# Query features made transposed and spread over the partitions by DMA, in place of transposes on TensorE

## The chip, the core and the metric

The kernel runs on one core of one Trainium2 chip. The metric is the device time of one execution in microseconds (us). Engines are named as the profile names them: PE is TensorE (PEld its weight loads), DVE is VectorE, ACT is ScalarE, POOL is GpSimd, and SP issues the DMAs (SPq is its queue).

## The reference

Three layers follow each other on 4 batches of 1088 rows: linear attention with 4 heads of 32, then two feed-forward blocks. The change touches the attention only:

```python
def phi(x):
    a = np.einsum('rd,bhsd->bhsr', S1, x)          # r = 8
    b = np.einsum('rd,bhsd->bhsr', S2, x)
    return np.einsum('bhsi,bhsj->bhsij', a, b).reshape(*x.shape[:-1], 64)
q_p, k_p = (phi(q), phi(k))
kv = np.einsum('bhsf,bhsd->bhfd', k_p, v);  z = np.sum(k_p, axis=2)
num = np.einsum('bhsf,bhfd->bhsd', q_p, kv)
den = np.einsum('bhsf,bhf->bhs', q_p, z)[..., None] + 1e-06
return num / den
```

Then `x` goes through `relu(xk @ w_k)**2 @ w_v`, gated by a sigmoid, and through a block with a 1088 x 1088 spatial product. All data are float32.

## The kernel before

**Chunks.** Each batch is cut into three chunks of 384, 384 and 320 rows, so there are 12 chunks, i = 0 to 11; batch b has the chunks 3b to 3b + 2. Work on a chunk's queries has four parts. `q_feat` (L229) makes the features: three matmuls (L188) with 128 rows of q each as the stationary operand give the 64 numbers a and b per row, ACT copies them out of PSUM (L191 or L196, shown by the profile as L114, the line of the helper), and DVE or POOL forms the 256 products a_i b_j (L199); the list `QP` gives chunks 3, 4, 6, 9 and 10 to POOL, the others to DVE. There a row of q lies on a partition and the features along it. `q_turn` (L233) turns that round: six transposes on PE against a unit matrix (L240) and two copies by ACT (L242) put features on partitions. `q_num` (L249) multiplies with the masked k-v sums (L257, six matmuls), divides (L261 to L263), and `q_out` (L266) transposes the result (L275) into the layout of the next layer.

**The loop.** The first feed-forward block runs in 96 steps g, eight for each chunk. Step g does `up(g)` (three matmuls, L336 by the helper at L111; Relu on ACT, L339; for even g the square on POOL, L342), `down(g - 4)` (L385 or L111) and `sqsplit(g - 1)` (ACT L371 or L359, DVE L117). A product in "three matmuls" splits both operands into a high and a low part; a plain float32 matmul (L385, L188, L257) shows as two records in the profile. All other work is hung on steps by `plan(g, fn)`: the four query parts of chunk j at `QS[j]` and after it, two steps apart, the key features and sums of a batch, `load_q`, `load_k`, and the loads and splits of the spatial weights wT (`wstep`: SP loads a 128 x 384 piece into one of two buffers `st0`, `st1`, ACT copies it and DVE or POOL subtracts, L117).

**Order.** The program is built with a scheduler that simulates a timeline and then writes each engine's queue in its own order. Each engine runs its queue strictly in that order and waits where an operand or a buffer isn't ready. So `plan` gives priorities, and the engine's row order is what counts. All DMAs go out from SP, so a transfer that waits for a buffer holds back each later one. PE has eight PSUM banks; the query parts use banks 4 to 7.

**Memory.** `VR` is one tile of nine pieces of 128 x 512. The query parts use pieces 0 to 5 of it (transposed features in 0 to 3, quotients in 4 and 5) until step 72, from which on the second block uses all of them. `n1L` holds the product of `q_feat`.

Of the kernel before, what the change touches and what calls it, by code (L numbers as in the profile page):

```python
# [8 lines left out]
F32 = mybir.dt.float32  # L9
# [3 lines left out]
ALU = mybir.AluOpType  # L13
# [29 lines left out]
KP = (6, 10)  # L43
QJ = (0, 0, 4, 1, 0, -4, -1, 0, 2, 2, 0, -8)
PG = 1
ES = 93
EP = 2
G2 = 96
# [18 lines left out]
def attn_moe_gmlp(ctx: ExitStack, tc: tile.TileContext, qT, kT, va, st, wk, wv, wr, win, wout,  # L67
                  wT, wtail, btail, mu, ident, msk, out):
    nc = tc.nc
    TE, VE, SE, GE = nc.tensor, nc.vector, nc.scalar, nc.gpsimd  # L70

    pool = ctx.enter_context(tc.tile_pool(name="sb", bufs=1))
    pp = ctx.enter_context(tc.tile_pool(name="ps", bufs=1, space=PSUM))

    uid = [0]

    def sb(tag, shape, dt=F32):
        uid[0] += 1
        return pool.tile(shape, dt, tag=tag, bufs=1, name=f"{tag}_{uid[0]}")
# [7 lines left out]
    def rot(*tags):  # L87
        i = count.get(tags, 0)
        count[tags] = i + 1
        return tags[i % len(tags)]  # L90
# [117 lines left out]
    def k_sum(b, g, ts=range(NT)):  # L208
# [12 lines left out]
        if g == 1:  # L221
# [4 lines left out]
                                         .to_broadcast([128, 2 * nh, HD + 1]), op=ALU.mult)  # L226
            kbd[b] = kb.rearrange("p (g h) c -> p g (h c)", g=2)

    def q_feat(i):  # L229
        qp = qst[i] = sb("n1L", [128, 3, 256])  # L230
        features(q_s[i // 3], i % 3, qp, 4, GE if i in QP else None)

    def q_turn(i):  # L233
        c = i % 3
        n = CH[c][1]
        qp, qt = qst[i], []
        for g in range(2):
            pt = bank(6 + g)
            for t in order3(c):
                TE.transpose(pt[:, cut(c, t)], qp[:, t, 128 * g:128 * g + 128], idn)  # L240
            q2 = vr(rot(0, 1, 2, 3), CMAX)
            copy(q2[:, :n], pt[:, :n])  # L242
            qt.append(q2)
        qst[i] = qt
# [396 lines left out]
    def plan(g, fn, *a):  # L641
        todo.setdefault(g, []).append(lambda: fn(*a))

    def gated(fn):
        return wraps(fn)(lambda *a: behind(prep_0, fn, *a))
# [4 lines left out]
    for j in range(1, NI):  # L650
        sp = 1 if j < 3 else 2
        for n, fn in enumerate((q_feat, q_turn, q_num, q_out)):
            plan(QS[j] + sp * n, gated(fn) if j < 3 and n == 0 else fn, j)
        e = QS[j] + 3 * sp
        plan(max(8 * j - 6, e + 1), prep, j)
        plan(max(8 * j - 4, e + 2), prep_r, j)
        plan(8 * j - 2, receive, j)
        plan(8 * j - 1, gate, j)
# [23 lines left out]
    def conv_late():  # L682
        behind(anchor[:1], conv64)

    for n in range(3):
        plan(R0[n], conv_first)
        if n < 2:
            plan(R0[n], total_wv, n)
# [122 lines left out]
```

## Time and profile before

| | |
|---|---|
| three runs | 474.23, 474.27 and 476.06 us, median 474.27 |
| profiled execution, whole | 475.52 us |
| its span, first to last instruction | 473.7 us |
| granted clock of TensorE, mean | 0.995 of full speed |
| PE busy over the span | 456.4 us (96%) |
| DVE, ACT, POOL busy | 235.6, 236.3, 189.9 us |
| hardware DMA queue | 12192 packets, 18.31 MB |

The span is shown by the profile in 40 slices and can be asked for stretch by stretch. It has three stages: the start with the first key features (0 to 40 us), the loop of 96 steps beside the remaining attention (40 to about 215 us), and the spatial products (215 us to the end). A group's row names a line, an engine and an operation, then output and input tiles. Matmuls overlap in the records, so PE's busy time is no sum of durations: the pace of PE is read from the starts of neighbouring rows, or from the chain that ended last, which counts each piece once.

### The profile page before, as it was taken

Reading aid. Unit: us, or ns where it says so; the run is one execution under the profiler, and the core shown is the slowest. Engines: PE = TensorE matmul, PEld = TensorE weight load, DVE = VectorE, ACT = ScalarE, POOL = GpSimd, SP = SyncE. Lnnn points to the kernel's source line nnn. Section 1 sums busy time; section 2 is a strip of 40 time slices with the busy share of each in tenths; the row PEclk is TensorE's granted clock in tenths of the full one; section 3 lists DMA queues with packets and bytes.
Section 4 is the critical chain, followed back from the end, with each engine's and each line's share of the span. In section 5 each row is a group of like instructions: output and inputs, shape, how many; then the busy total and the mean of one; then the engine's idle time right before and its main releaser. Section 6 shows DMA issues by size and latency. Waiting matters only on the chain.

```text
span 473.7 us, 7304 instructions
## 1 busy us (share of the span) xinstructions
PE 456.4 (96%) x2754; PEld 433.4 (91%) x2754; DVE 235.6 (50%) x433; ACT 236.3 (50%) x569; POOL 189.9 (40%) x247
## 2 busy tenths in 40 slices
PE   6987999989999999999999999999999999999997
PEld 5976899788998898899999999999999999999996
DVE  3778748788477774437552335621335521212121
ACT  2464687886786866876435423432523442311111
POOL 2447545576475785456325503341213440200000
PEclk9899999999999999999999999999999999999999
DMA  7952200112200000022000000000100000100001
GB/s 239 335 192 91 92 1 19 33 35 77 66 19 0 2 0 1 0 72 80 26 17 18 0 15 0 1 2 0 48 1 1 1 1 0 48 1 0 1 1 47
DMA packets 12228, 18.77 MB, mean 40 GB/s; under 512 B 1761, under 2 KB 10785, under 8 KB 12193
## 3 DMA queue, kind: packets, MB, share of 16 engines
q1 hardware_dynamic: 12192, 18.31, 12.3%
q8 instruction: 21, 0.34, 0.3%
q14 instruction: 15, 0.11, 0.1%
HBM read 16.08 MB, written 2.23 MB: 39 GB/s over the span
## 4 chain that ended last, share of the span: by engine, by line
PE 71%; DVE 9%; ACT 6%; DMA 5%; POOL 4%; issue 3%; SPq 1%; POOLq 0%; DVEq 0%; ACTq 0%
PE p L111 59%; DMA st<-in_wT_dram 3%; PE p L385 3%; DVE w L117 3%; PE p L219 2%; PE p L257 2%; PE p L507 2%; PE p L508 2%; ACT m L339 2%; DMA xs0H<-in_va_dram 2%; PE p L188 1%; DVE w L127 1%; ACT w L114 1%; DVE m L117 1%; ACT w L371 1%
## 5 line engine op out<-in xcount | busy, mean ns | idle before, releaser
L512 DVE TENSOR_TENSOR m<-p,m 128x384 f32<-128x384 f32 (+1 forms) x43 | 22.9, 532 | 96.9 <-PE p L508 92.7
L111 PE MATMUL p<-m,k 128*128 128x384 f32 (+1 forms) x288 | 65.4, 347 | 2.7 <-ACT m L339 2.7
L342 POOL TENSOR_TENSOR m<-m 128x384 f32<-128x384 f32 (+1 forms) x48 | 41.3, 863 | 46.9 <-ACT m L339 43.2
L499 ACT ACTIVATE m<-p 128x384 f32<-128x384 f32 (+1 forms) x44 | 20.6, 469 | 77.2 <-PE p L111 73.4
L111 PEld LDWEIGHTS p<-m,k 128*128 128x128 f32 x288 | 47.8, 189 | 6.9 <-ACT m L339 3.7
L111 PE MATMUL p<-w,m 128*128 128x384 f32 (+1 forms) x288 | 52.3, 327 | 0.0
L111 PE MATMUL p<-w,k 128*128 128x384 f32 (+1 forms) x288 | 51.6, 327 | 0.0
L111 PE MATMUL p<-w,n1H 128*128 128x384 f32 (+1 forms) x192 | 48.7, 330 | 1.0 <-DVE x L512 1.0
L111 PEld LDWEIGHTS p<-w,m 128*128 128x128 f32 x288 | 48.1, 188 | 0.5
L111 PE MATMUL p<-w,n0H 128*128 128x384 f32 (+1 forms) x192 | 48.2, 329 | 0.0
L111 PEld LDWEIGHTS p<-w,k 128*128 128x128 f32 x288 | 47.9, 188 | 0.3
L339 ACT ACTIVATE m<-p 128x384 f32<-128x384 f32 (+1 forms) x96 | 42.9, 473 | 9.5 <-PE p L111 8.9
L117 DVE TENSOR_TENSOR w<-m,w 128x384 fp32r<-128x384 f32 (+1 forms) x44 | 33.4, 771 | 26.5 <-ACT w L371 21.7
L117 DVE TENSOR_TENSOR m<-m,m 128x384 fp32r<-128x384 f32 (+1 forms) x47 | 27.2, 578 | 28.8 <-ACT m L114 27.6
L111 PEld LDWEIGHTS p<-w,n1H 128*128 128x128 f32 x192 | 34.2, 188 | 2.4 <-DVE x L512 1.3
L453 POOL TENSOR_SCALAR rs<-mv 128x1 f32<-128x1 f32 x34 | 8.4, 246 | 66.0 <-DVE mv L452 65.1
L111 PEld LDWEIGHTS p<-w,n0H 128*128 128x128 f32 x192 | 34.2, 188 | 0.5
L385 PE MATMUL p<-w,wvT 128*128 128x384 f32 (+1 forms) x88 | 34.5, 474 | 0.1
L447 ACT ACTIVATE VR<-p 128x512 f32<-128x512 f32 x34 | 20.2, 597 | 27.7 <-PE p L111 27.6
L111 PE MATMUL p<-w,n0L 128*128 128x384 f32 (+1 forms) x96 | 31.5, 328 | 0.0
L111 PE MATMUL p<-w,n1L 128*128 128x384 f32 (+1 forms) x96 | 31.5, 328 | 0.0
L455 DVE TENSOR_SCALAR VR<-VR,mv,rs 128x512 f32<-128x512 f32 x34 | 21.1, 621 | 20.4 <-POOL rs L454 20.4
(193 smaller groups left out, 1042.9 us busy)
## 6 DMA issues: line engine op xcount, KB each, us to landing
st<-in_wT_dram SPq DMA_DIRECT2D x16, 192.0 KB, 2.4
w<-in_kT_dram SPq DMA_DIRECT2D x8, 192.0 KB, 4.5
w<-in_qT_dram SPq DMA_DIRECT2D x8, 192.0 KB, 3.9
out_dram<-m SPq DMA_DIRECT2D x8, 192.0 KB, 1.9
st<-in_wT_dram SPq DMA_DIRECT2D x8, 160.0 KB, 2.3
xs0H<-in_va_dram SPq DMA_DIRECT2D x2, 528.0 KB, 7.0
xs0L<-in_va_dram SPq DMA_DIRECT2D x2, 528.0 KB, 4.4
w<-in_wk_dram SPq DMA_DIRECT2D x2, 512.0 KB, 6.2
```

Of the source, the lines that this page charges most:

```text
L111: TE.matmul(out_ap, lhsT=l, rhs=r, start=first and n == 0, stop=last and n == 2)
L117: return eng.tensor_tensor(out=L, in0=src, in1=H.bitcast(F32), op=ALU.subtract)
L219: TE.matmul(kv[:, w * g:w * g + w], lhsT=kp, rhs=vt if wide else vt[:, VP * g:VP * g + VP], start=(t == 0), stop=(t == NT - 1))
L257: nd_pe[0] = TE.matmul(o.rearrange("p h c -> p (h c)"), lhsT=qt[g][:, cut(c, t)], rhs=kb[:, g], start=not wide or g == 0, stop=not wide or ...
L339: SE.activation(out=r, in_=hk, func=AF.Relu)
L342: anchor[2] = GE.tensor_tensor(out=sq, in0=r, in1=r, op=ALU.mult)
L385: TE.matmul(vvs[i], lhsT=wvT[:, f // 2], rhs=hls.pop(g), start=f == 0, stop=f == NF - 1)
L447: SE.activation(out=v, in_=pv, func=AF.Relu)
L455: VE.tensor_scalar(out=v, in0=v, scalar1=mv[:, 0:1], scalar2=rs, op0=ALU.subtract, op1=ALU.mult)
L499: SE.activation(out=u, in_=pu, func=AF.Relu)
L507: TE.matmul(acc, lhsT=T2, rhs=wtile(NK, c)[1], start=False, stop=False)
L512: VE.tensor_tensor(out=u, in0=acc, in1=u, op=ALU.mult)
```

## The change

For chunks 3 to 11 (`SPREAD = 3`; batches 1 to 3) `q_feat` becomes `q_spread` and `q_turn` becomes `q_prod`; chunks 0 to 2 stay as they were. `q_order` copies the feature matrix once on POOL into an order by factor and head, so that one matmul with it as the stationary operand and the chunk's q as the moving one gives all a and b with their index on the partitions. ACT copies 96 of these rows into piece 8 of `VR`. SP writes them to DRAM (`far0` or `far1`), then reads them back six times with repeated rows: two transfers fill `fa` (each row of a eight times), four fill `fb` (the eight rows of b eight times). `q_prod` multiplies the two tiles in one instruction on POOL or DVE, by the same list `QP`. `fa` lies in pieces 0 and 1 or 2 and 3 of `VR`, `fb` in pieces 6 and 7 or in `n1L`, by turns. Chunks 3 to 9 have `q_spread` two steps earlier than `q_feat` was (`QE_ = 2`).

```diff
--- before.py
+++ after.py
@@ -43,6 +43,8 @@
 KP = (6, 10)
 QJ = (0, 0, 4, 1, 0, -4, -1, 0, 2, 2, 0, -8)
 PG = 1
+SPREAD = 3
+QE_ = 2
 ES = 93
 EP = 2
 G2 = 96
@@ -71,6 +73,8 @@
 
     pool = ctx.enter_context(tc.tile_pool(name="sb", bufs=1))
     pp = ctx.enter_context(tc.tile_pool(name="ps", bufs=1, space=PSUM))
+
+    dp = ctx.enter_context(tc.tile_pool(name="dr", bufs=1, space=bass.MemoryType.DRAM))
 
     uid = [0]
 
@@ -226,11 +230,48 @@
                                          .to_broadcast([128, 2 * nh, HD + 1]), op=ALU.mult)
             kbd[b] = kb.rearrange("p (g h) c -> p g (h c)", g=2)
 
+    Sq = [None]
+
+    def q_order():
+        t = sb("T12", [128, 2, 2 * NH, 8])
+        for x in range(2):
+            GE.tensor_copy(t[:, x], Sb[:, :, 8 * x:8 * x + 8])
+        Sq[0] = t.rearrange("p s h i -> p (s h i)")
+
+    def q_spread(i):
+        b, c = divmod(i, 3)
+        o, n = CH[c]
+        e = rot(1, 0)
+        pq = bank(6 + e)[:, :n]
+        TE.matmul(pq, lhsT=Sq[0], rhs=q_s[b][:, o:o + n], start=True, stop=True)
+        y = vr(8, n)[:96]
+        copy(y, pq[:96])
+        fa = VR[:, 2 * e:2 * e + 2, :n]
+        fb = VR[:, 6:8, :n] if e else sb("n1L", [128, 2, n])
+        far = dp.tile([96, n], F32, tag=f"far{e}", bufs=1, name=f"far_{i}")
+        nc.sync.dma_start(out=far, in_=y)
+        for h in range(NH):
+            r, g = 8 * h, h // 2
+            if h % 2 == 0:
+                nc.sync.dma_start(out=fa[:, g], in_=far[r:r + 16].unsqueeze(1).to_broadcast([16, 8, n]))
+            nc.sync.dma_start(out=fb[64 * (h % 2):64 * (h % 2) + 64, g],
+                              in_=far[64 + r:72 + r].unsqueeze(0).to_broadcast([8, 8, n]))
+        qst[i] = (fa, fb)
+
+    def q_prod(i):
+        fa, fb = qst[i]
+        (GE if i in QP else VE).tensor_tensor(out=fa, in0=fa, in1=fb, op=ALU.mult)
+        qst[i] = [fa[:, 0], fa[:, 1]]
+
     def q_feat(i):
+        if i >= SPREAD:
+            return q_spread(i)
         qp = qst[i] = sb("n1L", [128, 3, 256])
         features(q_s[i // 3], i % 3, qp, 4, GE if i in QP else None)
 
     def q_turn(i):
+        if i >= SPREAD:
+            return q_prod(i)
         c = i % 3
         n = CH[c][1]
         qp, qt = qst[i], []
@@ -650,7 +691,8 @@
     for j in range(1, NI):
         sp = 1 if j < 3 else 2
         for n, fn in enumerate((q_feat, q_turn, q_num, q_out)):
-            plan(QS[j] + sp * n, gated(fn) if j < 3 and n == 0 else fn, j)
+            early = QE_ if SPREAD <= j < 10 and n == 0 else 0
+            plan(QS[j] + sp * n - early, gated(fn) if j < 3 and n == 0 else fn, j)
         e = QS[j] + 3 * sp
         plan(max(8 * j - 6, e + 1), prep, j)
         plan(max(8 * j - 4, e + 2), prep_r, j)
@@ -682,6 +724,7 @@
     def conv_late():
         behind(anchor[:1], conv64)
 
+    plan(QS[SPREAD] - QE_ - 3, q_order)
     for n in range(3):
         plan(R0[n], conv_first)
         if n < 2:
```

In the built order the first place is PE behind the first Relu-square steps, about 40 to 47 us of the trace before. Before (`n1L_548` holds the product of chunk 3, `w_83` the q of batch 1, `kb` the k-v sums, `w_100` and so on the squares):

```order
L257 MATMUL p_164_585<-kb_54_209,VR_61 128x132 x6
L240 MATMUL p_170_612<-idn_62,n1L_548 128x128 x3
L240 MATMUL p_171_617<-idn_62,n1L_548 128x128 x3
L188 MATMUL p_203_712<-Sbd_119,w_83_320 128x128 x3
L385 MATMUL p_110_414<-w_100_379,wvT_79 128x384
L111 MATMUL p_110_414<-w_105_398,xs1L_78 128x384
L111 MATMUL p_110_414<-w_105_398,xs1H_77 128x384 x2
L385 MATMUL p_110_414<-w_111_418,wvT_79 128x384
L111 MATMUL p_110_414<-w_120_447,xs1L_78 128x384
L111 MATMUL p_110_414<-w_120_447,xs1H_77 128x384 x2
```
After (`T_116` is the ordered feature matrix, `w_83` and `w_155` the q of batches 1 and 2):

```order
L246 MATMUL p_188_674<-w_83_322,T_116_430 128x384
L192 MATMUL p_208_749<-Sbd_121,w_154_564 128x128 x3
L316 MATMUL p_106_403<-idn_64,VR_63 128x128 x3
L246 MATMUL p_206_737<-w_83_322,T_116_430 128x320
L115 MATMUL p_110_416<-w_92_348,xs1L_80 128x384
L115 MATMUL p_110_416<-w_92_348,xs1H_79 128x384 x2
L246 MATMUL p_275_975<-w_155_568,T_116_430 128x384
L298 MATMUL p_163_593<-kb_54_211,VR_63 128x132 x6
L192 MATMUL p_255_908<-Sbd_121,w_154_564 128x128 x3
L426 MATMUL p_110_416<-w_100_381,wvT_81 128x384
```
The six transposes and three feature matmuls of a chunk have gone, and the single matmuls of chunks 4, 5 and 6 (each on line 246) now stand close together, far ahead of the `kb` products that need them.

The second place is SP, from the second load of `win` on. Before (`wT` pieces go into `st`):

```order
L147 DMA w_205_719<-in_win_dram 128x1024
L147 DMA w_252_877<-in_win_dram 128x1024
L147 DMA w_288_998<-in_wout_dram 128x1024
L173 DMA w_237_828<-in_qT_dram 128x384 x2
L173 DMA w_237_828<-in_qT_dram 128x320
L412 DMA st_365_1247<-in_wT_dram 128x384
L412 DMA st_349_1204<-in_wT_dram 128x384
L412 DMA st_387_1323<-in_wT_dram 128x384
L412 DMA st_420_1418<-in_wT_dram 128x384
L412 DMA st_455_1530<-in_btail_dram 128x384
```
After (`far_513` belongs to chunk 3, `far_678` to chunk 4):

```order
L151 DMA w_201_722<-in_win_dram 128x1024
L252 DMA far_513<-VR_63 96x384
L151 DMA w_242_865<-in_win_dram 128x1024
L256 DMA VR_63<-far_513 128x1x384
L257 DMA VR_63<-far_513 64x1x384 x2
L256 DMA VR_63<-far_513 128x1x384
L257 DMA VR_63<-far_513 64x1x384 x2
L252 DMA far_678<-VR_63 96x384
L177 DMA w_229_825<-in_qT_dram 128x384 x2
L177 DMA w_229_825<-in_qT_dram 128x320
L256 DMA VR_63<-far_678 128x1x384
L257 DMA n1L_677<-far_678 64x1x384 x2
```
Between the two loads of `win` and behind them stand now the write and the six reads of each chunk in turn; the q of batch 3 (`w_229`) is loaded between chunk 4's write and its reads.

The third place is SP further on, among the `wT` loads. Before:

```order
L412 DMA st_401_1364<-in_wT_dram 128x384
L412 DMA st_576_1938<-in_wT_dram 128x384
L412 DMA st_436_1470<-in_wT_dram 128x384
L412 DMA st_589_1977<-in_wT_dram 128x384
L427 DMA st_575_1935<-in_wtail_dram 64x384
L412 DMA st_606_2033<-in_wT_dram 128x384
L412 DMA st_583_1960<-in_wT_dram 128x384
```
After (`far_1502` is chunk 9, `far_1640` chunk 11, `far_1661` chunk 10, `far_1358` chunk 8):

```order
L453 DMA st_350_1233<-in_wT_dram 128x384
L257 DMA VR_63<-far_1502 64x1x384
L252 DMA far_1640<-VR_63 96x320
L252 DMA far_1661<-VR_63 96x384
L256 DMA VR_63<-far_1358 128x1x320 x2
L453 DMA st_337_1198<-in_wT_dram 128x384
L257 DMA n1L_1639<-far_1640 64x1x320 x4
L453 DMA st_370_1300<-in_wT_dram 128x384
L256 DMA VR_63<-far_1502 128x1x384
L453 DMA st_402_1399<-in_wT_dram 128x384
L256 DMA VR_63<-far_1502 128x1x384
L453 DMA st_436_1513<-in_btail_dram 128x384
```
The `wT` loads that followed each other now stand between reads that fill `VR` or `n1L` and so wait for an earlier chunk to have left its buffer.

The fourth place is POOL, at the first products. Before:

```order
L199 TENSOR_TENSOR n1L_548<-sab_553 128x768
L680 TENSOR_TENSOR wvT_79<-xs1H_77,xs1L_78 128x256
L296 TENSOR_TENSOR m_112_420<-x_59_232 128x384
L680 TENSOR_TENSOR wvT_79<-xs1H_77,xs1L_78 128x256
L199 TENSOR_TENSOR n0H_564<-sab_569 128x768
L199 TENSOR_TENSOR n1L_711<-sab_716 128x768
L117 TENSOR_TENSOR xrL_453<-mx_450,xrH_452 128x384
L342 TENSOR_TENSOR m_162_578<-m_161_576 128x384
```
After:

```order
L337 TENSOR_TENSOR m_112_422<-x_59_234 128x384
L722 TENSOR_TENSOR wvT_81<-xs1H_79,xs1L_80 128x256
L263 TENSOR_TENSOR VR_63<-VR_63 128x2x384
L121 TENSOR_TENSOR xrL_458<-mx_455,xrH_457 128x384
L263 TENSOR_TENSOR VR_63<-VR_63,n1L_677 128x2x384
L383 TENSOR_TENSOR m_161_586<-m_160_584 128x384
L121 TENSOR_TENSOR xrL_474<-mx_471,xrH_473 128x384
L383 TENSOR_TENSOR m_144_529<-m_143_527 128x384
```
The products of chunks 3 and 4 (line 263) stand behind the sums `wvT` and ahead of the squares (lines 342 before, 383 after).

## Rows read from the trace of the kernel before

**Rows 1.** Stretches: length, then busy PE, PEld, DVE, ACT, POOL, clock, DMA share, GB/s
```profile
40.00:150.00 110.00, 105.27 (x678) 94.20 (x677) 78.65 (x130) 81.46 (x205) 65.80 (x64) 1.00 0.14 41
...
215.00:473.70 258.70, 255.44 (x1518) 251.48 (x1516) 91.95 (x184) 86.85 (x201) 66.58 (x97) 1.00 0.04 14
```

**Rows 2.** PE's waits from 36 to 160 us: total, times, longest
```profile
PE p L111 <- ACT m L339: 2.7, 4, 1.3
PE p L275 <- DVE VR L263: 1.6, 2, 1.4
PE p L188 <- ACT sab L114: 0.9, 1, 0.9
PE p L240 <- POOL n1L L199: 0.7, 1, 0.7
```

**Rows 3.** The chain that ended last: start, us, work and count
```profile
101.20 0.65 PE p L240 x6
101.85 0.67 PE p L188 x6
102.70 0.65 PE p L385 x2
...
125.66 0.54 PE p L385 x2
```

**Rows 4.** PE in order of time, 42 to 64 us: start, us, work
```profile
42.67 0.87 PE L240 MATMUL p<-idn,n1L 128*128 128x128 f32 x6 [0.67 <-POOL n1L L199]
44.41 0.94 PE L188 MATMUL p<-Sbd,w 128*128 128x128 f32 x6 [0.86 <-ACT sab L114]
...
56.55 1.55 PE L257 MATMUL p<-kb,VR 128*128 128x66 f32 x12
...
62.87 1.45 PE L257 MATMUL p<-kb,VR 128*128 128x66 f32 x12
```

**Rows 5.** ACT groups by line, 40 to 150 us: busy, mean ns, idle before
```profile
L114 ACT ACTIVATE VR<-p 128x384 f32<-128x384 f32 (+1 forms) x18 | 8.0, 475 | 0.7 <-PE p L240 0.7
...
L114 ACT ACTIVATE sab<-p 128x192 f32<-128x192 f32 x6 | 2.0, 331 | 0.0
L114 ACT ACTIVATE bs<-p 128x96 f32<-128x96 f32 x8 | 2.0, 247 | 0.0
```

**Rows 6.** Line 199, the outer product, by engine: ns min, median, max
```profile
L199 DVE TENSOR_TENSOR n1L<-p,bs x7: 944/950/958, 13.4 to 117.1; 128x768 f32<-128x768 f32 x7
L199 POOL TENSOR_TENSOR n1L<-sab x5: 1506/1760/1835, 41.1 to 137.9; 128x768 f32<-128x768 f32 x5
```

**Rows 7.** ACT, POOL and the DMA queue (SPq) in order of time
```profile
34.59 0.78 ACT L125 ACTIVATE w<-w,ebias 128x512 int32<-128x512 int32 x1
...
44.36 0.73 POOL L680 TENSOR_TENSOR wvT<-xs1H,xs1L 128x256 f32<-128x256 f32 x1
...
51.68 0.99 POOL L117 TENSOR_TENSOR xrL<-mx,xrH 128x384 fp32r<-128x384 f32 x1
...
36.09 2.58 SPq L147 DMA_DIRECT2D w<-in_win_dram  x2
```

**Rows 8.** DMA issues, KB each, median us to landing; issue time, ns min/median/max; queue
```profile
st<-in_wT_dram SPq DMA_DIRECT2D x16, 192.0 KB, 2.4
...
out_dram<-m SPq DMA_DIRECT2D x8, 192.0 KB, 1.9
...
w<-in_qT_dram SPq DMA_DIRECT2D x4, 160.0 KB, 5.0
...
q1 hardware_dynamic: 12192, 18.31, 12.3%
...
L173 SPq DMA_DIRECT2D w<-in_qT_dram x12: 328/428/498, 3.5 to 56.2; - x12
```

**Rows 9.** ACT's wait for wT loads, 40 to 200 us, and one instance
```profile
ACT w L114 <- DMA st<-in_wT_dram: 7.2, 6, 1.8
...
100.41 0.79 PE L111 MATMUL p<-m,k 128*128 128x384 f32 x3 [1.33 <-ACT m L339]
```

## The prediction

> **What bounds the kernel now.** I read the busy times by stretch first, then PE's own waits, then the chain that ended last, and last the engines and SP's queue in order of time around the first chunks that the change touches. In the loop of steps, 40 to 150 us, PE is busy 105.27 of 110 us at the full clock, ACT 81.46, DVE 78.65, POOL 65.80, and the DMA engines 14% [rows 1]. The reader is to see that PE is the only engine there without room, and that its idle time, 4.7 us, is less than what one part of the change takes from it. PE's waits between 36 and 160 us sum to 5.9 us in the four largest groups: 2.7 for a Relu on ACT, 1.6 for quotients, 1.6 for the features of a query chunk (0.9 for an ACT copy and 0.7 for a product on POOL) [rows 2]. From 215 us on nothing that the change touches is at work; those 258.70 us stay [rows 1].
>
> **What PE loses and gets, chunk by chunk.** The chain counts each piece of PE's work once, so its rows are prices: six transposes 0.65 us, six records of three feature matmuls 0.67, together 1.32. The new matmul is plain float32 over 384 or 320 columns in two records, as line 385 is: 0.65 or 0.54 [rows 3]. So a chunk of 384 saves 0.67 and one of 320 saves 0.78. Six of the nine chunks have 384 and three have 320: 4.0 + 2.3 = 6.4 us with the rounding. This lies on PE in the stretch that PE bounds, so I count all of it.
>
> **ACT.** Per chunk two copies of 0.475 us and one of 0.247 or 0.331 give way to one copy of 96 x 384 [rows 5]. Taken at 0.475 (a copy of as many columns), that is about 0.75 us less, times nine 6.8 us less on ACT. ACT isn't the bound, so this counts only through PE's 2.7 us of waits for Relu [rows 2]: between 0 and 2.7, and I take 0, because these waits come from other things too (below).
>
> **Waits that go.** Chunk 3's transposes waited 0.67 us for POOL's product and the feature matmuls behind them 0.86 for ACT's copy [rows 4]. Both instructions are gone. Next late there is what stands behind on PE, the products of the second block, which come from ACT and DVE; so I count 1.0 of the 1.6.
>
> **Product on DVE and POOL.** It has 768 elements a partition before and after; it took 0.95 us on DVE and 1.51 to 1.84 on POOL [rows 6]. The new operands are plain pieces of SBUF, a form that no row shows; up to 0.3 either way by the spread of POOL's rows, hidden beside 44 idle us of POOL and 31 of DVE in the stretch [rows 1]. The two small copies of `q_order` have 64 elements each, on a POOL that needs 0.73 for 256 [rows 7]: under 1.5 us, far ahead of their use, taken as nothing.
>
> **The round trip through DRAM, added.** What waits for it are `q_prod` on POOL or DVE and, behind it, line 257 on PE. SP serves the chunks one after the other, so chunks 3, 4 and 5, whose matmuls stand close together, are where it can be late. The trace has no such round trip; I bound it with the issue time (0.33 to 0.43 us), the landing of a write to DRAM (1.9 us), and two loads, 2.4 us for a quiet one and 5.0 for one among others [rows 8].
> Start: ACT's copy of chunk 3 stands behind the conversion that begins at 34.59 and takes 0.78, so it ends near 35.9; SP's first `win` load goes at 36.09, the write behind it at 36.5, and the second `win` load is through at 38.67 [rows 7].
> Low side (0.33, 1.9, 2.4): write 3 lands at 38.4, its six reads go from 38.7 to 40.7, write 4 lands at 42.6, three q loads pass meanwhile, reads 4 go until 44.6 and land at 46.7. POOL has by then finished `wvT` (44.36 + 0.73 = 45.1 [rows 7]), then chunk 3's product (1.51), a subtraction (0.99 [rows 7]) and chunk 4's product: ready at 49.1. Write 5 lands at 46.5, its reads go behind the `wout` load until 48.9 and land at 51.0; with 0.95 on DVE 51.9.
> High side (0.43, 5.0, 5.0): reads 4 land at 56.3, product ready at 58.0; reads 5 land at 63.9, ready at 64.9.
> Wanted: the products of chunks 4 and 5 began at 56.55 and 62.87 before [rows 4]. PE arrives earlier by what it has saved until then, 2 x 0.67 + 1.5 and 2.1 + 1.5: at 53.7 and 59.3.
> So PE waits between 0 (with 4.6 and 7.4 us to spare) and 5.6 us. With 14% of the DMA engines in use the quiet rows are nearer; I take 1.5. Behind the waiting POOL instruction stand a subtraction and the squares of line 342, behind DVE's the product `x` of line 389, and PE's step waits for these four steps later; that is inside the 1.5. Later chunks have many steps between their matmul and their use.
>
> A rule of the Trainium skill speaks against this, "DMA: Bandwidth & Descriptors", on why a DMA increments its semaphore by 16: a transfer uses the largest number of engines up to 16 that divides the slowest dimension of both sides, so the four reads with eight rows outermost would use eight. No row here shows such a read. The queue's 12192 packets took 12.3% of 16 engines over 473.7 us [rows 8], 76 ns each; a chunk's 512 packets are 2.4 us on sixteen engines, and by the rule 48 on the busier eight, 3.7 us. By that each round is 1.2 us longer and the third chunk 3.7 later: the low side is still in time, and a middle case would wait 1.5 + 2.4 to 3.7, and the sum would be up to 3.7 us higher.
>
> **SP's queue, moved.** Each `wT` load of the loop is now behind some of the 63 new transfers. SP needs 63 x 0.33 to 0.43 = 21 to 27 us to issue them, in a stretch where it has time. But a read that fills `VR` or `n1L` waits until the chunk before has left it, and the `wT` loads behind wait too. ACT waits for these loads already, 7.2 us in six cases, the longest 1.8; behind one of these PE stood 1.33 for a Relu [rows 9]. Bounds: ACT's waits may fall to 0 (ACT has 6.8 us less to do but reaches the loads sooner), or each of some ten loads may show its landing of 2.4, 24 us. On PE at 1.33 of 1.8, that is from -5 to +12. I take +1.5: a load goes at most one chunk's reads later.
>
> **Sum.** -6.4 - 1.0 + 1.5 + 1.5 = -4.4. The profiled execution took 475.52 (span 473.7 and 1.8 around it), 1.25 above the median of the three runs, 474.27. 475.5 - 4.4 = 471.1; against the median **469.9 us**.
>
> **Rivals.**
> *The round trips are late.* The high side holds, PE waits 5.6 instead of 1.5. For it: three chunks in a row through one queue, with 1.5 MB of `win` and `wout` among them. Against: the share of 14%. 469.9 + 4.1 = 474.0, no change. By the rule of the Trainium skill on eight engines it would come to nearly the same, 469.9 + 3.7 = 473.6.
> *It doesn't do what it says.* The loop's pace is set by the ring Relu, square, subtraction, product with its four steps of lag, and PE's time is only refilled with waiting. Against: PE waits 2.7 us for Relu in 124 us [rows 2], so the ring is mostly ahead. Then only the lost waits count: 474.27 - 1.0, 473.3.
> *The wT loads are held back; slower.* Place: SP, where the loads of `st` stand behind reads that wait for the `kb` products of chunks 6 to 9. Each load shows 1.5 to 2 us of landing on ACT, ten of them 15 to 20 in place of 7.2; ACT is in order, so the Relu is late, and PE pays 1.33 of 1.8: 0.74 x 10.3 = 7.6 instead of 1.5. 469.9 + 6.1 = 476.0, at the high bound 480. It decides from the point where ACT's waits for `st` pass 7.2 + 5.9 / 0.74 = 15 us: there the 5.9 that the other terms leave is gone.
> *All of it comes in.* No new wait, the 1.6 in full and half of the waits for Relu: -6.4 - 1.6 - 1.4 = -9.4, 464.9.
>
> **How the numbers follow.** The forecast has a chance of 0.50, with its own range of 467.5 to 472; late round trips 0.15; no effect of PE's time 0.07; wT loads 0.21; all of it 0.07. From these the range is 466.0 to 478.5: it leaves out most of the last case and the far end of the wT case. 0.5% is 2.4 us, about what three runs can tell from no change. Faster than 471.9: 0.07 + nine tenths of the forecast, and a little of the others, 0.55. Within 0.5%: the two middle cases and a tenth of the forecast, 0.25. Slower than 476.6: four fifths of the wT case and the end of the late round trips, 0.20.
>
> **What would show it.** Right: the new matmul at 0.65 and 0.54 in the chain; PE's busy share in the stretch from 40 us on as high as now and the stretch some 4 to 6 us shorter; the stretch of the spatial products unchanged; POOL's and DVE's waits for the reads short. Wrong: PE's line 257 waiting for line 263 of chunks 4 and 5 by more than 2 us; ACT waiting over 15 us for `st`; the time from the first read's issue to the last landing above 6 us; the time lost from 215 us on.

## The result, and the profile after

| | median, us | range | runs |
|---|---|---|---|
| before, beside it | 474.37 | 474.16 to 476.06 | 6 |
| after | 478.78 | 476.72 to 480.28 | 6 |

The ratio is 1.0084, with an interval of 1.0056 to 1.0113: slower by 0.8%, where 469.9 was forecast, and outside the range by 0.3 us. The profiled execution took 476.72 us (span 474.9) and is the fastest of the six; its mean granted clock was 0.999. The other five lay between 478.05 and 480.28 at mean clocks of 0.985 to 0.993. So the two profiles compared below are only 1.2 us apart, where the medians are 4.4: that of before lies 1.2 above its median, that of after 2.1 below, and there is no trace of the slower executions with the lower clocks.

The stretches of the profile after, with the columns of [rows 1]:

```profile
40.00:150.00 110.00, 96.76 (x570) 82.40 (x571) 74.23 (x131) 74.79 (x180) 65.08 (x65) 1.00 0.36 110
...
215.00:474.90 259.90, 256.58 (x1523) 252.41 (x1522) 93.08 (x184) 87.51 (x203) 67.40 (x97) 1.00 0.04 13
```

The totals of its page (busy time, share of the span, instructions) and its DMA queue (packets, MB, share of 16 engines):

```profile
PE 451.2 (95%) x2664; PEld 423.7 (89%) x2664; DVE 234.5 (49%) x433; ACT 232.3 (49%) x551; POOL 193.2 (41%) x249
...
q1 hardware_dynamic: 18384, 26.25, 17.5%
```

Between 40 and 150 us PE is busy for 8.5 us less than in [rows 1], and it isn't done sooner: it stands idle for 13.2 us instead of 4.7. Over the span PE's busy time fell by 5.2 us (456.4 to 451.2) and its idle time rose by 6.4 (17.3 to 23.7). The last product `x` of the first block began at 223.10 us, before at 221.58; from there to the end it took 251.8 and 252.1 us. So all that this execution loses is lost before the end of the first block, and the waits below put it in the loop.

Where the idle time comes from: waits from 36 to 160 us after (total, times, longest), of [rows 2] and [rows 9]:

```profile
ACT VR L118 <- DMA far<-VR: 12.3, 7, 2.7
...
ACT w L118 <- DMA st<-in_wT_dram: 4.7, 6, 1.6
...
PE p L246 <- ACT VR L118: 4.1, 4, 2.1
...
PE p L115 <- ACT m L380: 2.8, 3, 2.1
...
POOL VR L263 <- DMA n1L<-far: 2.5, 1, 2.5
ACT w L118 <- DMA st<-in_btail_dram: 2.4, 1, 2.4
PE p L115 <- DVE x L430: 2.1, 2, 1.1
...
PE p L426 <- ACT w L400: 1.9, 2, 1.5
```

The first row is new. ACT's copy of a chunk (L118 into `VR`) waits until the write of the chunk before has read the one `y` buffer, and all that ACT has behind it waits too; PE's matmul L246 waits for the PSUM bank that this copy frees. ACT's waits for `st` are what they were, 4.7 + 2.4 against 7.2 [rows 9]. (Over the whole span they are 15.8 us in both kernels: the expectation of e1_y2 below sets 15.8 of the whole span after beside 7.2 of 40 to 200 us before.)

SP's queue in order of time, chunks 4 and 5 after (start, us, instruction):

```profile
43.90 0.72 SPq L252 DMA_DIRECT2D far<-VR  x1
44.72 1.34 SPq L177 DMA_DIRECT2D w<-in_qT_dram  x3
47.69 0.56 SPq L256 DMA_DIRECT2D VR<-far  x1
48.30 1.22 SPq L257 DMA_DIRECT2D n1L<-far  x2
49.64 0.55 SPq L256 DMA_DIRECT2D VR<-far  x1
50.23 1.21 SPq L257 DMA_DIRECT2D n1L<-far  x2
51.94 0.34 SPq L252 DMA_DIRECT2D far<-VR  x1
...
54.67 0.62 SPq L257 DMA_DIRECT2D VR<-far  x1
```

The issue of a spreading read takes 0.55 to 0.6 us, and SP stands between write and first read until the write has landed, so a chunk occupies the queue for 7.5 us (from 43.90 to 51.44; in chunk 4's case three loads of q pass in the shadow of the landing). The chain that ended last runs along it (start, us, what), with a write's landing of 2.7 to 3.7 us in each piece shown (chunk 3's, ahead of the reads, took 4.15):

```profile
43.90 3.74 DMA far<-VR
48.21 0.91 PE p L246 x2
...
51.94 2.67 DMA far<-VR
54.67 0.62 SPq L257
...
65.18 3.69 DMA far<-VR
...
83.91 3.53 DMA far<-VR
```

And the consumers: PE's products with `kb` of chunks 4 and 5, at 56.55 and 62.87 before [rows 4], were forecast for 53.7 and 59.3 if nothing else held them:

```profile
57.08 1.45 PE L298 MATMUL p<-kb,VR 128*128 128x66 f32 x12
...
63.75 1.45 PE L298 MATMUL p<-kb,VR 128*128 128x66 f32 x12
```

### The profile page after: what moved, and what is told of

It reads as the page before. It is cut to its first block, busy times and chain, and to the rows that moved or that the text cites. A ratio compares the mean times of both kernels' runs of the same rounds, so it can differ in the third digit from the quotient of the medians.

```text
span 474.9 us, 7236 instructions
## 1 busy us (share of the span) xinstructions
PE 451.2 (95%) x2664; PEld 423.7 (89%) x2664; DVE 234.5 (49%) x433; ACT 232.3 (49%) x551; POOL 193.2 (41%) x249
## 4 chain that ended last, share of the span: by engine, by line
PE 67%; DMA 8%; DVE 8%; POOL 6%; ACT 4%; SPq 3%; issue 2%; POOLq 0%; ACTq 0%; DVEq 0%
PE p L115 59%; DMA far<-VR 5%; PE p L426 2%; DMA st<-in_wT_dram 2%; PE p L549 2%; PE p L548 2%; DVE w L121 2%; SPq L257 2%; DMA mus<-in_mu_dram 1%; PE p L298 1%; ACT m L380 1%; POOL rs L495 1%; POOL m L383 1%; DVE VR L496 1%; DVE w L132 1%
## 5 line engine op out<-in xcount | busy, mean ns | idle before, releaser
L115 PE MATMUL p<-m,k 128*128 128x384 f32 (+1 forms) x288 | 66.4, 348 | 4.4 <-ACT m L380 2.8
L115 PEld LDWEIGHTS p<-m,k 128*128 128x128 f32 x288 | 49.0, 188 | 10.9 <-ACT m L380 4.2
L383 POOL TENSOR_TENSOR m<-m 128x384 f32<-128x384 f32 (+1 forms) x48 | 42.6, 893 | 30.2 <-ACT m L380 30.1
L121 DVE TENSOR_TENSOR w<-m,w 128x384 fp32r<-128x384 f32 (+1 forms) x44 | 29.7, 688 | 29.0 <-POOL m L383 18.6
```

The costliest lines, as they stand in the source:

```text
L115: TE.matmul(out_ap, lhsT=l, rhs=r, start=first and n == 0, stop=last and n == 2)
L121: return eng.tensor_tensor(out=L, in0=src, in1=H.bitcast(F32), op=ALU.subtract)
L383: anchor[2] = GE.tensor_tensor(out=sq, in0=r, in1=r, op=ALU.mult)
```

## The experiments

Each ran beside the kernel before on the same chip. Ratio is to the kernel before, with its 95% interval; clock is the median of the runs' mean granted clock. The diffs show only the lines that matter. But for the h runs and w1_one8, the scheduler made a new row order for each kernel.

| run | what | median us | ratio | clock |
|---|---|---|---|---|
| e1_y2 | two y buffers | 479.29 | 1.0064 (1.0045 to 1.0083) | 0.989 |
| e2_write_act | write from ACT's queue | 479.46 | 1.0088 (1.0061 to 1.0115) | 0.998 |
| e4_spread6 | batches 2 and 3 alone | 477.25 | 1.0036 (1.0011 to 1.0060) | 0.996 |
| e5_nospread | no write, no reads | 473.88 | 0.9964 (0.9950 to 0.9978) | 0.993 |
| x2_write_only | no reads | 478.35 | 1.0049 (1.0027 to 1.0070) | 0.985 |
| x3_reads_only | no write | 477.27 | 1.0050 (1.0029 to 1.0072) | 0.987 |
| x1_twice | before, 54 transposes more | 481.90 | 1.0134 (1.0110 to 1.0157) | 0.996 |
| x1_third | before, 36 transposes fewer | 476.66 | 1.0030 (1.0014 to 1.0046) | 0.989 |
| h1_third | the same, order held | 474.08 | 0.9984 (0.9970 to 0.9998) | 0.996 |
| h2_nospread | e5's work, order held | 473.71 | 0.9995 (0.9974 to 1.0016) | 0.993 |
| r_one8 | before, one transpose more | 473.53 | 0.9977 (0.9965 to 0.9990) | 0.996 |
| r_one5 | before, one transpose more | 477.01 | 1.0055 (1.0031 to 1.0079) | 0.996 |
| w1_one8 | before's work in r_one8's order | 473.96 | 0.9983 (0.9964 to 1.0003) | 0.996 |
| h3_after | the change, before's order | 498.15 | 1.0473 (1.0429 to 1.0516) | 0.970 |
| h6_spread6 | batches 2 and 3, before's order | 489.05 | 1.0286 (1.0256 to 1.0316) | 0.981 |
| h6_nospread6 | the same, no write, no reads | 478.82 | 1.0079 (1.0055 to 1.0103) | 0.992 |

### Is it the buffer, the queue, or no DMA at all?

```diff
-        y = vr(8, n)[:96]                                       # e1_y2
+        y = sb(rot(m(8), m(9)), [128, CMAX])[:96, :n]
-        nc.sync.dma_start(out=far, in_=y)                       # e2_write_act
+        nc.scalar.dma_start(out=far, in_=y)
-SPREAD = 3                                                      # e4_spread6
+SPREAD = 6
```

> Edit: the 96-row copy that goes to DRAM gets two buffers of its own by turns (tiles that are free in the loop) in place of the one piece of VR. Theory 'one buffer': ACT waited 12.3 us in 7 copies for the write of the chunk before, Relu stood behind it, and PE paid about 8 us more idle time in the loop than before; with two buffers ACT's wait for these writes falls under 3 us, PE's idle time from 40 to 150 us from 13.2 to about 8, and the time from 478.8 to 472 to 474. Rival 'one queue': SP's serial round trips hold the wT loads, and ACT's waits there (15.8 us, before 7.2) decide; ACT's waits for writes fall too, but the time stays at 477 to 479. Rival 'order': the rearranged engine orders cost by themselves; no change beyond 1 us.

> Edit: the write to DRAM is issued from ACT's queue, right behind the copy, the reads stay on SP; one buffer as in the change. 'One buffer': what held the buffer was partly the write's place in SP's queue behind six reads (3.5 us); out of it, a write's landing of 2.7 to 4.2 us remains, so ACT's waits fall from 12.3 to 4 to 7 us, ACT pays nine issues of about 0.4, and the time falls to 475 to 477. 'One queue': SP loses only nine of 63 transfers and still waits for each landing, so 478 to 480. 'Order': 478 to 480.

> Edit: SPREAD = 6, so only batches 2 and 3 (six chunks) use the new path; chunks 3 to 5 keep transposes. PE's saving falls from 6.4 to 4.3 us. 'One buffer': the waits of ACT for writes were 1.5 and 1.9 and 2.7 us at the first chunks; about half of 12.3 goes, and the time is 475 to 477. 'One queue': the wT loads stand beside the same later chunks, so their waits stay and the time is 478 to 480, since the saving shrinks. 'Order': within 1 us of the change or of before, by chance.

```diff
-        nc.sync.dma_start(out=far, in_=y)                       # e5_nospread, and the six reads with it
-        (GE if i in QP else VE).tensor_tensor(out=fa, in0=fa, in1=fb, op=ALU.mult)
+        (GE if i in QP else VE).tensor_tensor(out=fa, in0=fb, in1=fb, op=ALU.mult)
```

> Edit: the write and the six reads of each chunk are left out, and q_prod multiplies a constant tile; matmul, ACT copy and product stay (the spread itself, and with it the right features, are left out). It is the worth of PE's and ACT's saving without DMA. 'One buffer' and 'one queue' alike: the waits go, PE's idle time is as before the change (4.7 us) or less and the time is 467 to 470. 'Order': the new orders alone eat the gain, 474 or more.

Two buffers brought ACT's wait for the write from 12.3 us in seven waits to 6.7 in five, and the time by nothing that the intervals can tell. The wait moved: the products (L263) now waited 11.1 us for transfers in place of 7.4 in the change (waits of e1_y2 from 36 to 160 us):

```profile
ACT m L118 <- DMA far<-m: 6.7, 5, 2.7
...
POOL VR L263 <- DMA w<-in_qT_dram: 3.8, 1, 3.8
POOL VR L263 <- DMA VR<-far: 3.8, 1, 3.8
...
DVE VR L263 <- DMA VR<-far: 3.5, 1, 3.5
```

ACT's queue for the write brought nothing either, and ACT's wait stayed, at 13.6 us in seven. Six of the nine chunks cost 0.0036 where nine cost 0.0084, but with these intervals and a new order in each kernel the share of a batch can't be read from that. Neither the buffer nor the write's place in SP's queue shows as the cause by itself, as far as kernels with different orders can tell; no one theory's figures fit all four runs, 'order' comes nearest. The telling run is e5: without any DMA the change gives 1.6 us (475.51 to 473.88), not the 7.4 of the forecast's first two terms. With the DMAs it is 4.4 us over the kernel before: together they cost 6.0, to within what the two orders add.

### Which half of the round trip?

x2_write_only is the changed kernel without the six reads, with the one buffer; x3_reads_only reads two DRAM tiles that are written once.

```diff
-        nc.sync.dma_start(out=far, in_=y)                       # x3_reads_only; far is written once in q_order
+        far = fars[e][:, :n]
```

> The changed kernel with the write of each chunk to DRAM, and without the six reads that spread it; the product is made of a constant tile, so the values are not the reference's. What is left of the spread is ScalarE's wait for the one y buffer (12.3 us in 7 waits in the changed kernel) and the write's issue on SP. Without write and reads the time was 473.9, with both 478.8 to 479.3. Theory 'one buffer': the wait stays, 477-478.5. Theory 'one queue' (reads hold SP, wT loads come late): 473.5-474.5. With fewer DMAs in flight a write should land faster, so the wait may be nearer 6 than 12 us.

> The changed kernel with the six spreading reads of each chunk, and without the chunk's write: they read two DRAM tiles that are written once, with a constant, before the first of them (so the values are not the reference's). Matmul and ScalarE's copy stay; nothing waits for the copy's buffer. What is left is six read issues on SP (about 3.5 us a chunk, 31 us in all) and their traffic, without SP's wait for the landing of the write. Theory 'one queue': wT loads are still late and the products wait for reads, 476.5-478. Theory 'one buffer': 473.5-474.5. If both halves stay under 475, it is their chain (write, landing, reads, one behind the other) that costs.

Both theories wanted one half near 474. Neither is: the halves cost 4.0 and 4.1 us over e5 by the ratios, both together 5.7. They don't add, so what they cost is no sum of their own waits, unless the orders, which differ here too, hide it.

### What is PE's time worth in this loop?

```diff
-                TE.transpose(pt[:, cut(c, t)], qp[:, t, 128 * g:128 * g + 128], idn)
+                for _ in range(2 if i > 2 else 1):              # x1_twice
+                    TE.transpose(pt[:, cut(c, t)], qp[:, t, 128 * g:128 * g + 128], idn)
-            for t in order3(c):                                 # x1_third
+            for t in order3(c) if i < 3 else (0,):
```

> The kernel before, with each of the 54 transposes of batches 1 to 3 (L240, six to a chunk) issued twice into the same bank; the result is the same and no DMA is added. The six transposes of a chunk took 0.65 to 0.67 us on TensorE, so 54 more are 5.9 us of its time. Theory 'TensorE's time counts in full' (the prediction's first term): the time rises by nearly all of it, to 480.5-481.5 beside 475.5 of the kernel before. Theory 'filled from the slack' (idle time of TensorE in the loop, 6.1 us between 40 and 215 us, takes it up): 477-478.5. Both allow for the 0.4 us spread of the kernel before.

> The kernel before, with two of three transposes of batches 1 to 3 left out: one of each group of three is made, and ScalarE's copy repeats its columns to the same width (so the values after it are not the reference's). ScalarE, VectorE, GpSimd and the queues have the same instructions; TensorE has 36 transposes fewer, 3.9 to 4.0 us by 0.65 us for six. Theory 'TensorE's time counts in full': 471.5 beside 475.5. Theory 'the saving is refilled with waiting' (the left-out-DMA kernel gave 1.6 us of 6.4): a quarter of it, 474.0-475.0.

This is the heart of the matter. 5.9 us of transposes more cost 6.4 by the ratio; 3.9 us fewer made the kernel 1.4 slower. In the scheduler's orders PE's time counted upwards in full and downwards not at all. x1_third's stretches show what goes with the loss (columns as in [rows 1]: after the two lengths PE, PEld, DVE, ACT, POOL, then the granted clock):

```profile
44.00:46.00 2.00, 0.82 (x7) 0.82 (x8) 2.00 (x5) 1.38 (x4) 2.00 (x4) 1.00 0.00 0
46.00:50.00 4.00, 4.00 (x13) 2.93 (x12) 3.38 (x8) 1.71 (x5) 1.38 (x1) 0.57 0.31 122
50.00:54.00 4.00, 4.00 (x28) 3.47 (x26) 1.64 (x4) 2.70 (x7) 3.35 (x3) 1.00 0.02 9
...
118.00:120.00 2.00, 0.03 (x1) 0.00 (x0) 1.04 (x2) 1.49 (x4) 0.00 (x0) 1.00 0.21 76
120.00:126.00 6.00, 5.30 (x30) 5.31 (x30) 3.42 (x6) 5.81 (x16) 4.48 (x5) 0.72 0.24 62
126.00:130.00 4.00, 4.00 (x34) 3.92 (x32) 1.19 (x2) 2.12 (x5) 2.13 (x3) 1.00 0.39 107
```

PE waits (0.82 busy of 2.00, then 0.03 of 2.00), and right behind each wait the clock stands between its levels of 2.4 and 1.2 GHz for the stretch: 0.57 over 4 us and 0.72 over 6 us, 0.43 x 4 = 1.7 us of full-speed time lost and 0.28 x 6 = 1.7 again. The kernel before has one such place in its profile, at 12 to 16 us (0.59). There an idle gap is paid once as a gap and once as clock.

The second suspect was the scheduler: taking transposes out moved some 80 of DVE's 431 rows and 200 of ACT's 562. The next two runs give every engine the row order of the kernel before by edges between neighbours that set the order and add no wait:

```diff
         attn_moe_gmlp(tc, *args)
+        hold(tc)        # each engine's instructions in the order of the kernel before
```

> The kernel before with 36 of the 54 transposes of batches 1 to 3 left out, as in the run called x1_third (values after them are not the reference's), but every engine now has exactly the order of the kernel before: in x1_third the scheduler had moved some 80 of VectorE's 431 and 200 of ScalarE's 562 rows. TensorE has 3.9 us less to do, beside 475.0 of the kernel before. Theory 'a new order' (the loss of x1_third came from another order, not from the lost work): 471-472.5. Theory 'refilled with waiting' (the other engines' chain sets the loop): 474-475. Theory 'idle time costs the clock' (a gap on TensorE lowers the granted clock): 475-477, with stretches of 0.91 in the loop as in x1_third.

> The changed kernel without the write and the reads (product of a constant tile, so values are not the reference's), in the order of the kernel before: the matmul of a chunk stands where the first feature matmul stood, ScalarE's copy where its copy stood, the product where the feature product stood, and the 18 copies and 54 transposes are gone. In its own order this gave 473.9 beside 475.5, 1.6 us of the 6.4 that TensorE's rows promise. Theory 'a new order': 468.5-470.5 beside 475.0. Theory 'refilled with waiting': 472.5-474. Theory 'idle time costs the clock': 473-475 with stretches under 0.95 in the loop.

With the order held, x1_third's loss of 0.3% became a gain of 0.2%: the order, with the clock that came with it, was worth 2 us there. But the gain is 0.8 of 3.9 us, and for h2 0.2 of 6.4, with an interval from a loss of 0.8 to a gain of 1.2 us (0.9 by the medians). The totals of h2's page:

```profile
PE 451.7 (96%) x2664; PEld 425.0 (90%) x2664; DVE 236.3 (50%) x433; ACT 232.6 (49%) x551; POOL 191.5 (41%) x250
```

Its span was 470.9, so that execution gained 2.8: PE's busy time fell by 4.7 and its idle time rose by 1.9, from 17.3 to 19.2. Its clock dipped once, as before's did: 0.72 over 6 us behind 0.58 us of idle (stretches, as above),

```profile
22.00:24.00 2.00, 1.42 (x13) 1.28 (x12) 1.37 (x2) 0.48 (x1) 2.00 (x2) 1.00 1.01 342
24.00:30.00 6.00, 6.00 (x37) 5.97 (x37) 2.49 (x4) 1.54 (x5) 1.79 (x3) 0.72 0.63 197
34.00:38.00 4.00, 1.23 (x8) 0.84 (x8) 4.00 (x8) 3.72 (x9) 1.24 (x2) 1.00 0.09 27
```

yet the larger gap from 34 to 38 us, 1.23 busy of 4.00, lies in a stretch at 1.00, and the clock stayed there behind it; the falls seen here follow a gap, but not every gap is followed by one. The theory 'idle time costs the clock' wanted the falls in the loop; here the fall lies ahead of it, and the change's own profile has 13.2 us of idle in the loop, one gap of 2.11 us among it, at a clock of 1.00. Over h2's twelve runs the time goes with the mean clock, on the mean 471.6 us at 1.0 (one run), 473.0 at 0.996 (four), 474.3 at 0.993 (four), 476.4 at 0.989 (three). h1 has 473.2 at 1.0 (three) and 475.4 at 0.988 to 0.989 (two). The kernel before, beside them on the same chip, has 474.2 at 0.998 and above (11 runs) and 475.1 below (20). So at full clock h2 is 2.6 us ahead, by one run, and at 0.996, where the kernel before has 474.9 (nine runs), 1.9 by four. Less than half of the 6.4 shows at an equal clock, and h2's lower clocks take most of that again; why the same kernel gets different clocks is not shown.

### What is a new order worth by itself?

```diff
+                for _ in range(2 if (i, g, t) == (8, 0, 0) else 1):     # r_one8; (5, 0, 0) in r_one5
                     TE.transpose(pt[:, cut(c, t)], qp[:, t, 128 * g:128 * g + 128], idn)
```

> The kernel before with one transpose of chunk 8 issued twice: 0.11 us more for TensorE, same result. The scheduler answers with another order in the loop (some 120 of ScalarE's 562, 45 of VectorE's 431, 50 of GpSimd's 246 rows stand elsewhere). If the order is worth nothing: 475.0-475.3. Theory 'a new order' (the order of the kernel before is a good draw and others are worse): 476-479. Two draws (this and the next) give an idea of the spread.

> The same with one transpose of chunk 5 issued twice, a second draw of the order (some 90 of ScalarE's, 60 of VectorE's, 20 of GpSimd's rows stand elsewhere). If the order is worth nothing: 475.0-475.3. Theory 'a new order': 476-479.

> Exactly the work of the kernel before, with no transpose added, in the order that the scheduler gave the kernel with one transpose of chunk 8 doubled (473.5 beside 474.6). Theory 'the order alone': 473.3-473.6, 0.2% under the kernel before. If the time falls back to 474.6, the earlier difference was not the order's.

0.11 us of work changed the time by -1.1 and +2.6 us by the ratios: two draws of the scheduler lie 3.7 us apart. Part of the +2.6 is clock. r_one5's profiled execution, 480.70 us and the slowest of its eight, was at half clock for some 10 us behind a wait (stretches, columns as above):

```profile
116.00:120.00 4.00, 2.37 (x13) 1.61 (x12) 1.65 (x4) 2.47 (x6) 1.35 (x2) 1.00 0.41 123
120.00:131.00 11.00, 10.93 (x44) 9.74 (x44) 4.72 (x8) 5.93 (x15) 3.60 (x5) 0.53 0.13 37
```

At mean clocks of 0.998 and above the means are 473.2 (r_one8, five runs), 474.2 (before, 11) and 476.0 (r_one5, three): -1.1 and +1.8. The work of the kernel before in r_one8's order (w1_one8) is at 0.9983, the same gain within its interval, which just reaches 1. With r_one8 itself it is the fastest version here that does the whole computation, and 0.2% is all there is. For r_one5's order no such run was made. So a term of one to two and a half us, of either sign, has to be allowed for in every comparison of this kernel in which the order isn't held, x1_twice and e5 included.

### The round trips with the order held

h3_after puts the whole change into the row order of the kernel before, with matmul, copy, write and reads placed ahead by hand; h6_spread6 does so for batches 2 and 3, with more lead; h6_nospread6 is h6_spread6 without its DMAs. The new rows stand where the kernel before was at these times of its trace:

```diff
         attn_moe_gmlp(tc, *args)
+        hold(tc)
```

For h3 these are, chunk by chunk from 3 to 11, 36.4, 39.6, 46, 61, 76, 88, 100.5, 128 and 116 us for ACT's copies and 46, 49.5, 55.8, 70.5, 86.1, 97.7, 110.3, 138.5 and 126 for the products; for h6, from chunk 6, 62, 76.5, 87, 99, 126 and 114, and 74, 89.5, 101, 115, 139.5 and 128.

> The whole change (same result as the reference) with two y buffers, in the order of the kernel before: each chunk's matmul and copy stand about 9 us ahead of its product (the chain write 0.4, landing 3, six reads 3.5, landing 2 us), the write and the reads on SP's queue between the wT loads, one load in the shadow of a write's landing where there is one; the products stand where the feature products stood, or up to 9 us later where the round trip can't be ready. Theory 'price of the round trips' (ScalarE's wait and SP's queue cost 4 to 5 us wherever they stand): 477.5-479 beside 474.6-475.0. Theory 'placement' (the scheduler put them too late and into the queue's way): 473.5-475, that of the run without write and reads (473.7), or a little over it.

> The change for batches 2 and 3 alone (six chunks; same result), two y buffers, all other instructions in the order of the kernel before. Matmul and copy of a chunk stand 12 us ahead of the product, the product 3 to 10 us after the place of the feature product it replaces (its use by TensorE is later still), and the round trip lies between the wT loads on SP's queue. In the scheduler's order the same six chunks gave 477.25 beside 475.5. TensorE has 6 x 0.67 = 4.0 us less. Theory 'price of the round trips': 476.5-478 beside 475. Theory 'placement': 473-475, as without DMA. Theory 'late costs': 480 and more, if a product still waits for its reads.

> The same order and work without the write and the reads (product of a constant tile, so values are not the reference's). Theory 'refilled with waiting': 473.5-474.5 beside 475, as h2_nospread. If it is at 475 or more, the products' later places cost by themselves, and the difference to h6_spread6 is what the DMAs cost.

h3_after missed both of its ranges; h6_spread6 came out as 'late costs' had it, and h6_nospread6 above 475, where the products' later places cost by themselves: 3.8 us, after the 4 us of PE's work that were taken away. With the DMAs it is 10.2 more. h3 and h6 don't tell what a well-placed round trip would cost, since mine were not well placed; they show what one late landing does. From the chain of h6_spread6 that ended last:

```profile
145.70 3.57 DMA n1L<-far
...
149.43 1.80 POOL VR L292
151.23 0.80 POOL m L412
...
152.05 0.50 ACT m L409
...
152.59 1.65 PE p L144 x4
```

PE in order of time there:

```profile
152.59 1.33 PE L144 MATMUL p<-m,k 128*128 128x384 f32 x3 [3.51 <-ACT m L409]
```

And the stretches around it, columns as before:

```profile
148.00:152.00 4.00, 1.05 (x5) 0.47 (x3) 0.52 (x1) 0.24 (x1) 2.57 (x3) 0.85 0.14 40
152.00:156.00 4.00, 3.41 (x9) 2.78 (x10) 1.89 (x2) 2.56 (x6) 2.58 (x4) 0.50 0.00 0
156.00:160.00 4.00, 4.00 (x23) 3.50 (x22) 1.79 (x5) 1.42 (x3) 0.71 (x1) 0.79 0.00 0
```

The read lands 3.57 us after its issue; POOL's product stands ahead of a square (L412), ACT's next Relu (L409) waits for the buffer that the square frees, and PE waits 3.51 us for the Relu; behind the gap the clock is at 0.50 and 0.79 for 8 us, 2.8 us of full-speed time more. PE has no row that names the DMA.

## Why the prediction was wrong

**The step that failed** is the first term: "This lies on PE in the stretch that PE bounds, so I count all of it", 6.4 us. With no DMA at all it came to 1.6 us in the scheduler's order and 0.2 in before's, the waits that go included. The price of the transposes was not the fault: x1_twice paid 6.4 for 5.9 by the same rows, in an order of its own. (The prices of the feature matmuls and of the new one were tested by no run of their own; PE's busy time fell by 4.7 us in h2's profile, not by 6.4, so a part of the 6.4 may be size.) The inference was: 4.7 us of idle in 110 says that PE is the bound for work that is added. It doesn't say how much of a saving comes through when work is taken away, and here it was a quarter at most in the measured medians. Where the rest goes is known in part: h2's idle time rose by 1.9 us, and its slower executions have the lower clocks; what the loop then waits for is open. The rival "it doesn't do what it says", with 0.07, named that outcome (473.3) and was held too low; the ring that it blamed was not shown to be the limit.

**Waits that go**, -1.0: e5, which loses these waits too, gained 1.6 in all, so at most that is left for both terms in its order.

**ACT** was sized rightly: its busy time from 40 to 150 us fell by 6.7 us (81.46 to 74.79); I took nothing for it, and no run shows more. **The product** took 1.82 to 2.17 us on POOL and 0.81 to 2.13 on DVE, so in one case 1.2 us longer than before, where I allowed 0.3.

**Round trips late**, +1.5, with the low and high sides: chunk 3's reads and product passed the mark of 6 us that I had named (SP and POOL in order of time after):

```profile
39.95 0.63 SPq L256 DMA_DIRECT2D VR<-far  x1
...
47.57 1.82 POOL L263 TENSOR_TENSOR VR<-VR 128x768 f32<-128x768 f32 x1 [3.62 <-DMA w<-in_qT_dram]
```

From the first read's issue to the product are 7.6 us. The row puts the end of POOL's wait down to a q load, but by the semaphores in the trace it was the last of the six reads, which landed at 47.45. PE's line 298, though, never waits for the product in a row; the waits stand upstream, at ACT's copies, PE's L246 and POOL's place in the queue. I had priced the DMA's consumers and not its producer: ACT waited up to 2.7 us for a write to leave its buffer (12.3 us in seven waits), and PE 4.1 us for the PSUM banks of copies not made. That these waits are what the DMAs cost is not shown: e1_y2 nearly halved ACT's, and the time stayed. I had also taken the quiet rows because of a DMA share of 14%, which is a mean over 110 us. From 38 to 60 us it was 0.28 before, and the round trips made it 0.66 (before, then after; columns of [rows 1]):

```profile
38.00:60.00 22.00, 19.52 (x133) 16.98 (x134) 16.93 (x30) 12.11 (x32) 14.29 (x13) 1.00 0.28 89
...
38.00:60.00 22.00, 18.66 (x108) 14.69 (x108) 13.05 (x26) 10.50 (x27) 13.43 (x12) 1.00 0.66 202
```

The issue of a read was taken at 0.33 to 0.43 us from other transfers [rows 8], and was 0.55 to 0.6.

**The rule of the Trainium skill** on how many engines a transfer uses ("DMA: Bandwidth & Descriptors", on why a DMA increments its semaphore by 16) holds here as far as the number of engines goes. Beside its data each transfer has packets of 4 bytes in the trace: the kernel before has 86 transfers and 1376 of them, 16 each, so I read one for each engine that a transfer uses. The queue's packets of x2_write_only, which has the writes alone, are

```profile
q1 hardware_dynamic: 13200, 19.57, 13.1%
```

1008 more than before [rows 8], nine writes of 96 rows and 16 small packets. The change has 5184 more than that, 576 a chunk: 512 of data and 64 small ones, which fits 16 for each of the two reads of `fa` and 8 for each of the four with eight rows outermost. What that costs in time is not shown, since no run changed the shape of the reads.

**wT loads held back**, +1.5, and the slower rival with 0.21: wrong in the mechanism, as far as ACT's waits show it. ACT waited 7.1 us for `st` between 40 and 200 us, as before, and not the 15 from which that rival decides. That its time, 476.0, came nearest is chance.

**The two DMA terms together** were +3.0; by e5 and the change they are 4.4 + 1.6 = 6.0. The 8.8 us between the forecast's -4.4 and the +4.4 that came are so 5.8 from PE's time and the waits (-7.4 against -1.6) and 3.0 from the DMAs, each to within the orders. What stays open is how the 6 divide: buffers and queue changed alone gave nothing, either half gave two thirds, and the order, redrawn in each of these kernels, moves the time by as much as such a part.

## What to carry to other kernels

A share of 96% told here what added work costs, and not what less work gives. Before work taken off an engine is counted as time, try the cheapest kernel that leaves just this work out (x1_third, one edit), in the old order too (h1_third), and look whether the time moves. Where a scheduler writes the order, change 0.1 us of work first and see how far the time moves: smaller differences than that can't be put down to the edit. A DMA that replaces compute is priced at both ends, with the buffer it reads from and what the copy into that buffer holds.

## What the runs showed that I had not expected

- An idle gap can cost granted clock: in x1_third, behind 1.2 and 2.0 us of idle in a stretch of 2 us, it was 0.57 over 4 us and 0.72 over 6, 1.7 us lost each time; h2's runs spread over 5.1 us, and go with the clock. Other gaps as long cost none, and e2_write_act took 478.78 us at a clock of 1.0, so the clock is not all of the loss.
- One 0.11 us transpose moved the time by -1.1 or +2.6 us, most likely by the order that the scheduler then wrote: the work of before in the first of these orders kept the gain (0.9983, up to 1.0003).
- The issue of a read that repeats rows over partitions takes SP 0.55 to 0.6 us; that of a q load had a median of 0.43 [rows 8].
- A write to DRAM, which landed in 1.9 us for the outputs of 192 KB [rows 8], took, at 144 or 120 KB, 2.7 to 3.7 us among the spreading reads.
- A read with eight rows outermost used eight of the 16 DMA engines, by its packets.
